# Gates turned and spread over ranks through DRAM, with a transposed down projection, in an attention and mixture-of-adapters kernel

## The chip, the cores and the metric

The kernel runs on one core of a Trainium2 chip. The metric is the device time of one execution in microseconds. Before the change it is 389.1 us, the median of three runs (388.85 to 389.68).

## What is computed

Attention of 49,152 queries over few keys, and then a mixture of eight low-rank adapters on the attention's output. Cut to what matters:

```python
B, N, C = 4, 12288, 128                      # q is (B, N, C), kv is (B, 384, 32, C)
kv_pool = kv averaged over 4 x 4 patches     # 96 x 8 = 768 keys for each of B
k = v = kv_pool @ w_sr
a = softmax(q @ k.T / sqrt(C))
x = (a @ v).reshape(B * N, C)

logits = x @ w_gate                          # E = 8 adapters of rank 16, A (E, C, 16), B (E, 16, C)
top two adapters of each row; w = softmax of their two logits
out = x + sum over the two of w * ((x @ A[e]) @ B[e])
```

## The kernel before

A chunk is 512 queries, taken as four groups of 128; there are 96 chunks, 24 for each of the four batches, and every constant below is of that size (`T = 512`, `S = 4`, `P = 128`, `E = 8`, `RK = 16`, `NB = 24`, `GC = 4`). Ranks and adapters together make 8 x 16 = 128, so all down projections are one 128 x 128 matrix `a_bf`, and all up projections one matrix `b_bf`.

The steps of one chunk, each cut to its core. Scores come with keys on partitions; attending brings queries to partitions. Every matmul, transposes too, is recorded under the helper's line (`L68`), so the profile tells them apart by tile names.

```python
def scores(k, r):        # three times a chunk: 2 x 512 columns, then exp on ScalarE
    ps = ps_s.tile([P, 2, T], FP32, tag="sg")
    for i in range(2):
        mm(ps[:, i], kfT[b][:, 2 * r + i], rhs, ...)
    keep(nc.scalar.activation(em[k][:, 2 * r:2 * r + 2], ps, AF.Exp, ...))

def attend(k, s):        # four times a chunk: 6 matmuls of 137 columns (values, logits, sum)
    ...                  # acc: a PSUM tile of a pool with one buffer

def normalize(k):        # DVE: xn = acc / sum, and so empties acc
def top(k):              # DVE: the eight logits sorted, four MAX8
def route(k0):           # GpSimd, for a pair of chunks: arg and mask of the two chosen

def gates(k0):
    n, eng, arg, mask = routed[k0]                      # eng is GpSimd
    keep(nc.scalar.activation(th, arg, AF.Tanh, bias=0.0, scale=0.5))
    w = gpool.tile([P, GC * S, 8], FP32, tag="gw")      # queries on partitions
    keep(eng.tensor_tensor(w[:, 0:n], th, mask, op=ALU.mult))
    keep(eng.tensor_tensor(w[:, 0:n], w[:, 0:n], mask, op=ALU.add))

def transposes(kx, kh, engine):     # x of one chunk and hg of another, in one PSUM tile
    ps = mtile([P, 2, S, P], BF16, name="tt_ps")
    ...                             # 4 transposes of xn[kx], 4 of hg[kh]
    copy to sb                      # 1024 elements, or 512 where one of the two is absent
    xT[kx], hgT[kh] = sb[:, 0], sb[:, 1]

def down(k):
    hp[k] = mtile([P, S, P], name="h_ps")
    for s in range(S):              # xT is stationary, a_bf moves: queries on partitions
        mm(hp[k][:, s], xT[k][:, s], a_bf, ...)

def gate(k):                        # DVE: hg = hp * gate, the gate repeated over 16 ranks
def up(k):                          # 4 matmuls, hgT stationary, b_bf moving
def finish(k):                      # DVE: d_ps + xn, then the output DMA on SyncE
```

`mtile` takes its tiles from a PSUM pool with two buffers: `tt_ps`, `d_ps`, `h_ps` and the tiles of the key preparation go round in it. The gates use that a softmax of two logits is a tanh of their difference; the factor 0.5 is in `a_bf`.

The slots 14 to 71 are software-pipelined by one function; before and after it stand hand-ordered lists that the change leaves alone. Each engine works in the order in which the program gives it instructions. One slot, in order (`sc` scores, `ga` gates, `nm` normalize, `tt` transposes, `fi` finish, `at` attend, `tp` top, `ro` route, `dn` down, `ge` gate, `lq` the transposing load of four chunks' q on SyncE, `kv` a load of the next batch's keys, `pr` and `pa` its preparation on TensorE and GpSimd, `cq` a cast of q in DRAM, issued by GpSimd after a small copy `late` that waits for an earlier `lq`):

```python
def slot(k):
    if k % GC == 0: lq k // GC + 1
    kv of the next batch (i < 12), cq k // GC + 2 (k % GC == 2)
    sc k 0
    ga k - 4                        # for the first chunk of a pair
    nm k - 2;  tt k - 6, k - 7;  sc k 1;  up k - 8;  fi k - 8
    at k - 1, 0;  tp k - 2;  ro k - 2   # ro after the second of a pair
    sc k 2;  dn k - 6;  ge k - 6
    pr of the next batch
    at k - 1, 1 to 3
    pa of the next batch
```

Of the kernel before, what the change touches and what calls it, by code (L numbers as in the profile page):

```python
# [10 lines left out]
FP32 = mybir.dt.float32  # L11
BF16 = mybir.dt.bfloat16
U16 = mybir.dt.uint16
FP16 = mybir.dt.float16
AF = mybir.ActivationFunctionType
ALU = mybir.AluOpType
# [4 lines left out]
def kernel(  # L21
# [10 lines left out]
    nc = tc.nc  # L32
    P = 128
    B, N, C = q.tensor.shape
    E, RK = 8, 16
# [3 lines left out]
    T = 512  # L39
    S = T // P  # L40
    GC = 4
# [7 lines left out]
    const = ctx.enter_context(tc.tile_pool(name="const", bufs=1))  # L49
# [6 lines left out]
    rpool = ctx.enter_context(tc.tile_pool(name="rpool", bufs=4))  # L56
    gpool = ctx.enter_context(tc.tile_pool(name="gpool", bufs=6))
    run = ctx.enter_context(tc.tile_pool(name="run", bufs=3))
    opool = ctx.enter_context(tc.tile_pool(name="opool", bufs=6))
    qdram = ctx.enter_context(tc.tile_pool(name="qdram", bufs=1, space=bass.MemoryType.DRAM))  # L60
    ps_s = ctx.enter_context(tc.tile_pool(name="ps_s", bufs=2, space=bass.MemoryType.PSUM))
    ps_a = ctx.enter_context(tc.tile_pool(name="ps_a", bufs=1, space=bass.MemoryType.PSUM))
# [2 lines left out]
    keep = tc.keep_in_program_order  # L65

    def mm(*a, **k):
        return keep(nc.tensor.matmul(*a, **k))  # L68

    def mtile(shape, dtype=FP32, name="mb"):  # L70
        return ps_m.tile(shape, dtype, tag="mb", name=name)
# [51 lines left out]
    for item in """  # L123
# [5 lines left out]
        at = [None if x == "-" else int(x) for x in at]  # L129
# [13 lines left out]
    id_f = const.tile([P, P], FP32)  # L143
# [24 lines left out]
    def one(pool):  # L168
        if pool == "mb":
            return mtile([P, T], name="tail_ps")  # L170
        if pool == "acc":
            return ps_a.tile([P, S, 256], FP32, tag="acc", name="acc").rearrange(
                "p a c -> p (a c)")[:, 0:T]
        return ps_s.tile([P, 2, T], FP32, tag="sg", name="sg")[:, 0]

    def move(engine, o, i):
        return keep(nc.scalar.copy(o, i) if engine == "A" else nc.vector.tensor_copy(o, i))
# [129 lines left out]
    em, acc, xn, xg, srt, gw = {}, {}, {}, {}, {}, {}  # L307
    tts, xT, hgT, hp, hg, dp = {}, {}, {}, {}, {}, {}
# [34 lines left out]
    def normalize_half(k, h):  # L343
        if ("r", k) not in xn:
            xn["r", k] = rpool.tile([P, S], FP32, tag="rinv", name="rinv")
        if k // GC not in xg:
# [5 lines left out]
            xn[k][:, 2 * h:2 * h + 2], a[:, :, 0:VC],  # L352
            ri.unsqueeze(2).broadcast_to([P, 2, VC]), op=ALU.mult)))

    sizes = [1, 1] + [2] * (NB * (B - 1) // 2 - 1) + [1] * NB
    first, size = {}, {}
    for n in sizes:
        k0 = len(first)
# [3 lines left out]
    def top(k):  # L362
        k0, m = first[k], k - first[k]
        if k0 not in srt:
            srt[k0] = rpool.tile([P, GC, S, 8], FP32, tag="srt", name="srt")
        for s in range(S):
            keep(nc.vector.max(srt[k0][:, m, s], xn[k][:, s, C:VC]))  # L367

# [2 lines left out]
    def route(k0):  # L371
        n = size[k0] * S
        eng = nc.gpsimd
        m0 = k0 % GC * S
        lg = xg[k0 // GC].rearrange("p m s c -> p (m s) c")[:, m0:m0 + n, C:VC]
        so = srt[k0].rearrange("p m s e -> p (m s) e")[:, 0:n]

        def over(i):
            d = rpool.tile([P, GC * S, 8], FP32, tag=f"over{i}", name=f"over{i}")[:, 0:n]
            keep(eng.tensor_tensor(  # L380
                d, lg, so[:, :, i].unsqueeze(2).broadcast_to([P, n, 8]), op=ALU.subtract))
            return d

        arg, mask = over(0), over(1)
        keep(eng.tensor_tensor(arg, arg, mask, op=ALU.add))
        keep(eng.tensor_scalar(mask, mask, 0.0, None, op0=ALU.is_ge))  # L386
        routed[k0] = (n, eng, arg, mask)

    def gates(k0):
        n, eng, arg, mask = routed[k0]  # L390
        th = rpool.tile([P, GC * S, 8], FP32, tag="th", name="th")[:, 0:n]
        keep(nc.scalar.activation(th, arg, AF.Tanh, bias=0.0, scale=0.5))  # L392
        w = gpool.tile([P, GC * S, 8], FP32, tag="gw", name="gw")
        keep(eng.tensor_tensor(w[:, 0:n], th, mask, op=ALU.mult))  # L394
        keep(eng.tensor_tensor(w[:, 0:n], w[:, 0:n], mask, op=ALU.add))  # L395
        gw[k0] = w
# [30 lines left out]
    def gate(k):  # L427
        k0, m = first[k], k - first[k]
        hg[k] = run.tile([P, S, P], BF16, tag="hg", name="hg")
        keep(nc.vector.tensor_tensor(  # L430
            hg[k].rearrange("p s (e r) -> p (s e) r", e=E),
            hp[k].rearrange("p s (e r) -> p (s e) r", e=E),
            gw[k0][:, m * S:(m + 1) * S].rearrange("p s e -> p (s e)")
            .unsqueeze(2).broadcast_to([P, S * E, RK]), op=ALU.mult))

    def up(k):
        dp[k] = mtile([P, S, C], name="d_ps")
        for s in range(S):
            mm(dp[k][:, s], hgT[k][:, s], b_bf, start=(s == 0), stop=(s == S - 1))
# [146 lines left out]

    def gates_here(k):
        th, mask = routed[k]
        gw[k] = gpool.tile([P, S, E], FP32, tag="gw1", name="gw1")
        keep(nc.vector.scalar_tensor_tensor(gw[k], th, 1.0, mask, op0=ALU.add, op1=ALU.mult))  # L590

    late = const.tile([P, 1], FP32)
    a_bf = const.tile([P, P], BF16)
    b_bf = const.tile([P, C], BF16)

    def adapters():
        keep(nc.vector.tensor_scalar(a_bf, a_f, 0.5, None, op0=ALU.mult))
        keep(nc.vector.tensor_copy(b_bf, b_f))

    def first_casts(watch):  # L600
        keep(nc.gpsimd.tensor_copy(late, watch))
        for g in range(2, 4):
            cast_q(g)
# [7 lines left out]
    def plan(b):  # L611
# [8 lines left out]
        "k2": project_k, "va": project_v, "vb": copy_v, "tu": turn_v,  # L620
        "cs": lambda w: first_casts(q_f[1][:, 15, 0:1]),
        "cab": adapters,
        "lq": load_qT, "cq": next_cast,
        "kv": lambda b, h, r: load_kv(b, h, r, None),
        "pa": lambda b, n: plan(b)[0][n // 8][n % 8](),
        "pr": lambda b, n: plan(b)[1][n](),
        "sc": scores, "at": attend, "nm": normalize, "tp": top, "ro": route, "ga": gates,
        "tt": lambda x, h, e: transposes(x, h, nc.scalar if e == "A" else nc.vector),
        "dn": down, "up": up,
        "ge": lambda k: gate(k) if len(hp[k].shape) == 3 else gate_part(k, 0, S),  # L630
        "fi": lambda k: finish(k) if len(dp[k].shape) == 3 else add_here(k, 0, S),
        "nh": normalize_half, "xb": hold_x, "xt": turn_x, "cx": fetch_x, "hb": hold_h, "ht": turn_h, "ch": fetch_h,
        "o95": hold_acc, "pt": attend_part, "hd": hold_hp, "dn2": down_into, "ge2": gate_part,
        "db": hold_d, "up2": up_part, "af": add_here, "ca": carry, "pd": add_there,
        "lastroute": route_here, "lt": tanh_here, "lg_": gates_here,
    }

    def follow(order):
# [7 lines left out]
    def slot(k):  # L646
        b, i = divmod(k, NB)
        o = []
        if k % GC == 0 and k // GC + 1 < B * NG:
            o.append(f"lq {k // GC + 1}")  # L650
        i0 = 4 if b == 0 else 0
        if b + 1 < B and i0 <= i < i0 + 12:
            o.append(f"kv {b + 1} {(i - i0) // 4} {(i - i0) % 4}")
        if k % GC == 2 and k // GC + 2 < B * NG:
            o.append(f"cq {k // GC + 2}")
        o.append(f"sc {k} 0")
        if first[k - 4] == k - 4:
            o.append(f"ga {k - 4}")
        o += [f"nm {k - 2}", f"tt {k - 6} {k - 7} V", f"sc {k} 1", f"up {k - 8}", f"fi {k - 8}",
              f"at {k - 1} 0", f"tp {k - 2}"]  # L660
        if first[k - 2] + size[k - 2] - 1 == k - 2:
            o.append(f"ro {first[k - 2]}")
        o += [f"sc {k} 2", f"dn {k - 6}", f"ge {k - 6}"]
        prs = (14, 15, 16, 18, 19, 20, 21, 22, 23) if b == 0 else (11, 12, 13, 17, 18, 19, 21, 22, 23)
        if b + 1 < B and i in prs:
            o.append(f"pr {b + 1} {prs.index(i)}")
        o += [f"at {k - 1} {s}" for s in range(1, S)]
        if b + 1 < B and i % 2 == 0 and (8 if b == 0 else 6) <= i <= 20:
            lo, n = ((0, 3, 7, 10, 14, 17, 21)[(i - 8) // 2], 4 if i % 4 else 3) if b == 0 else (
                (i - 6) // 2 * 3, 3)  # L670
            o += [f"pa {b + 1} {m}" for m in range(lo, lo + n)]
        return "; ".join(o)
# [28 lines left out]
    for k in range(14, 72):  # L701
        follow(slot(k))
# [89 lines left out]
```

The softmax here doesn't subtract the row's maximum and nothing guards it: scores larger than these inputs give would overflow.

## Time and profile before

| | before |
|---|---|
| time, median of 3 | 389.1 us |
| span of the profiled run | 387.5 us |
| granted TensorE clock | 0.998 |
| queue of SyncE and its share of the 16 DMA engines | 63.98 MB, 55.8% |
| transposes of hg into tt_ps | 316 |
| multiplies by the gate in the slots, each | 0.691 us, 58 of them |
| copies out of tt_ps of 1024 and of 512 elements, each | 0.691 and 0.419 us |

The span is a little shorter than the time of an execution. Busy time is a sum of instruction times; matmuls are pipelined, so that their recorded durations overlap, and the pace of TensorE is read from the starts of successive groups. A wait row names who waited, and what came last of the things it waited for.

### The profile page before, as it was taken

The page shows a single profiled execution, that of the slowest core. Times are in us where ns is not written, and L with a number is a line of the kernel's source. Part 1 is how long each engine was busy: PE and PEld are TensorE (multiplying, and loading weights), DVE is VectorE, ACT ScalarE, POOL GpSimd, SP SyncE. Part 2 cuts the span into 40 slices and gives each one's busy share as a digit, 9 for nine tenths or more (in the row PEclk, how much of TensorE's full clock was granted, in tenths as well). Part 3 has the DMA queues.
Part 4 walks back from the last instruction along what each step waited for, and adds up shares of the span by engine and source line. Part 5 has one row for each costly group of instructions (what it writes and reads, how often), then busy time and mean ns, then how long its engine had stood idle before and what let it go on. Part 6 is the DMA issues. An engine that isn't in the chain of part 4 may idle for free.

```text
span 387.5 us, 11812 instructions
## 1 busy us (share of the span) xinstructions
PE 378.9 (98%) x4620; PEld 303.8 (78%) x4620; DVE 313.5 (81%) x973; ACT 308.3 (80%) x401; POOL 211.0 (54%) x474
## 2 busy tenths in 40 slices
PE   7899999999999999999999999999999999999994
PEld 4777788888888887888887887888877778788893
DVE  1445688989888888989988889888877687988896
ACT  1688997777687786877788787786879999998964
POOL 0011768987331768777533586877613234545682
PEclk9999999999999999999999999999999999999999
DMA  7998997975596999985579989856745665532245
GB/s 263 413 267 200 295 201 220 285 164 140 136 314 140 255 227 331 234 172 142 119 191 272 305 206 333 200 138 142 156 113 105 128 150 165 111 92 105 81 165 219
DMA packets 70745, 76.47 MB, mean 197 GB/s; under 512 B 49857, under 2 KB 51393, under 8 KB 70337
## 3 DMA queue, kind: packets, MB, share of 16 engines
q1 hardware_dynamic: 69552, 63.98, 55.8%
q0 software_dynamic: 704, 11.54, 17.1%
q8 instruction: 36, 0.59, 0.6%
q10 hardware_dynamic: 432, 0.20, 0.2%
q14 instruction: 21, 0.16, 0.2%
HBM read 50.53 MB, written 36.70 MB: 225 GB/s over the span
## 4 chain that ended last, share of the span: by engine, by line
PE 82%; DMA 8%; POOL 5%; DVE 1%; ACT 1%; issue 1%; SPq 0%; POOLq 0%; DVEq 0%; ACTq 0%
PE acc L68 32%; PE sg L68 29%; PE tt_ps L68 8%; DMA kvr<-in_kv_dram 6%; PE h_ps L68 4%; PE d_ps L68 3%; PE tail_ps L68 3%; DMA qT<-qbf 2%; POOL osb L562 1%; PE v_ps L68 1%; POOL over L380 1%; PE kpT_ps L68 1%; POOL gw L394 1%; ACT em L319 1%; POOL gw L395 1%
## 5 line engine op out<-in xcount | busy, mean ns | idle before, releaser
L319 ACT ACTIVATE em<-sg 128x1024 f16<-128x1024 f32 x288 | 278.3, 1026 | 56.4 <-PE sg L68 55.9
L68 PE MATMUL sg<-qT,kfT 128*128 128x512 bf16 x576 | 169.6, 379 | 0.0
L68 PE MATMUL acc<-vx,em 128*128 128x137 f16 x2280 | 168.9, 223 | 0.0
L68 PEld LDWEIGHTS <-em 128*128 128x128 f16 x2304 | 147.2, 98 | 11.4 <-DVE xn L337 2.7
L68 PEld LDWEIGHTS <-tts 128*128 128x128 bf16 x660 | 49.2, 98 | 31.8 <-issue 0.2
L264 POOL TENSOR_TENSOR kvr<-kvr 128x512 f32<-128x512 f32 x54 | 67.4, 1271 | 0.0
L337 DVE TENSOR_TENSOR xn<-acc,rinv 128x544 f32<-128x544 f32 x83 | 60.1, 724 | 3.2 <-DVE rinv L333 0.3
L380 POOL TENSOR_TENSOR over<-xn,srt 128x64 f32<-128x64 f32 (+1 forms) x114 | 29.8, 282 | 55.2 <-DVE srt L367 55.2
L416 DVE COPY tts<-tt_ps 128x1024 bf16<-128x1024 bf16 (+1 forms) x83 | 53.9, 651 | 4.8 <-PE tt_ps L68 4.6
L394 POOL TENSOR_TENSOR gw<-th,over 128x64 f32<-128x64 f32 (+1 forms) x57 | 16.7, 293 | 63.7 <-ACT th L392 62.7
L68 PEld LDWEIGHTS <-kfT 128*128 128x128 bf16 x576 | 46.1, 98 | 2.8
L430 DVE TENSOR_TENSOR hg<-h_ps,gw 128x512 bf16<-128x512 f32 x58 | 40.1, 691 | 4.5
L68 PEld LDWEIGHTS <-xn 128*128 128x128 bf16 x384 | 28.6, 98 | 18.2
L443 DVE TENSOR_TENSOR osb<-d_ps,xn 128x512 f32<-128x512 f32 x58 | 40.1, 691 | 0.0
L333 DVE RECIPROCAL rinv<-acc 128x4 f32<-128x4 f32 x83 | 15.1, 182 | 29.3 <-PE acc L68 28.6
L68 PE MATMUL tt_ps<-id_bf,xn 128*128 128x128 bf16 x344 | 33.3, 219 | 0.0
L367 DVE MAX8 srt<-xn 128x8 f32<-128x8 f32 x368 | 33.0, 152 | 0.1
L68 PE MATMUL tt_ps<-id_bf,hg 128*128 128x128 bf16 x316 | 30.4, 219 | 0.0
L68 PEld LDWEIGHTS <-hg 128*128 128x128 bf16 x384 | 25.6, 98 | 1.9 <-DVE hg L531 0.3
L68 PE MATMUL h_ps<-a_bf,tts 128*128 128x128 bf16 x264 | 25.5, 219 | 0.0
L68 PE MATMUL d_ps<-b_bf,tts 128*128 128x128 bf16 x260 | 25.1, 219 | 0.0
L386 POOL TENSOR_SCALAR over<-over 128x64 f32<-128x64 f32 (+1 forms) x57 | 19.1, 335 | 5.2
(119 smaller groups left out, 325.3 us busy)
## 6 DMA issues: line engine op xcount, KB each, us to landing
out_dram<-osb SPq DMA_DIRECT2D x91, 256.0 KB, 3.3
kvr<-in_kv_dram SPq DMA_DIRECT2D x45, 512.0 KB, 6.2
qbf<-in_q_dram POOLq DMA_DIRECT2D x22, 512.0 KB, 6.3
kvr<-in_kv_dram SPq DMA_DIRECT2D x6, 256.0 KB, 8.6
out_dram<-osb SPq DMA_DIRECT2D x9, 128.0 KB, 2.1
qf<-in_q_dram SPq DMA_DIRECT2D x4, 256.0 KB, 6.9
qf<-in_q_dram SPq DMA_DIRECT2D x2, 512.0 KB, 8.2
qT<-qbf SPq DMA_TRANSPOSE x22, 5.1
```

The costliest lines, as they stand in the source:

```text
L68: return keep(nc.tensor.matmul(*a, **k))
L264: keep(nc.gpsimd.tensor_tensor(u[:, lo:hi], u[:, lo:hi], v[:, lo:hi], op=ALU.add))
L319: keep(nc.scalar.activation(em[k][:, 2 * r:2 * r + 2], ps, AF.Exp, bias=0.0, scale=scale))
L333: keep(nc.vector.reciprocal(ri, acc[k][:, :, VC]))
L337: keep(nc.vector.tensor_tensor(x, acc[k][:, :, 0:VC], ri.unsqueeze(2).broadcast_to([P, S, VC]), op=ALU.mult))
L367: keep(nc.vector.max(srt[k0][:, m, s], xn[k][:, s, C:VC]))
L380: keep(eng.tensor_tensor(d, lg, so[:, :, i].unsqueeze(2).broadcast_to([P, n, 8]), op=ALU.subtract))
L386: keep(eng.tensor_scalar(mask, mask, 0.0, None, op0=ALU.is_ge))
L394: keep(eng.tensor_tensor(w[:, 0:n], th, mask, op=ALU.mult))
L416: keep(nc.vector.tensor_copy(sb[:, lo:hi], ps[:, lo:hi]))
L430: keep(nc.vector.tensor_tensor(hg[k].rearrange("p s (e r) -> p (s e) r", e=E), hp[k].rearrange("p s (e r) -> p (s e) r", e=E), gw[k0][:, m ...
L443: keep(nc.vector.tensor_tensor(osb, dp[k], xn[k][:, :, 0:C], op=ALU.add))
```

## The change

For 20 chunks, 30 to 41 and 54 to 61, the adapter's inner vector is produced with ranks on partitions from the start, so that it needs no transpose between the two projections. `a_bf` becomes stationary and the transposed x moves through it, in one matmul of 512 columns. The gate then has to lie with ranks on partitions too, and each adapter's gate has to be repeated over 16 partitions. GpSimd writes the gates of a pair as fp16 in the order adapter, group; TensorE transposes them (64 rows); VectorE copies them out; one DMA puts them to DRAM (16 KB); and a second DMA reads each of the eight rows 16 times into 128 partitions (256 KB). A turned chunk's x is transposed one slot later than before, and its output comes in the same slot as before.

```diff
+    turned = {*range(30, 42), *range(54, 62),}
 def gates(k0):
+        if k0 in turned:
+            keep(eng.tensor_tensor(th, th, mask, op=ALU.mult))
+            gh[k0] = gpool.tile([P, E, n], FP16, tag=f"gh{n}", name="gh")
+            keep(eng.tensor_tensor(gh[k0].rearrange("p e m -> p m e"), th, mask, op=ALU.add))
+            return
...
+    def turn_gates(k0, pool, engine):
+        ps = one(pool).bitcast(FP16)[0:n, 0:P]
+        mm(ps, gh[k0].rearrange("p e m -> p (e m)"), id_h, is_transpose=True, start=True, stop=True)
+        gt[k0] = rpool.tile([P, P], FP16, tag="gt", name="gt")[0:n]
+        move(engine, gt[k0], ps)
+
+    def put_gates(k0):
+        gd[k0] = gdram.tile([E, size[k0] * T], FP16, tag=f"gd{size[k0]}", name="gd")
+        keep(nc.sync.dma_start(gd[k0].rearrange("e (m t) -> (e m) t", t=P), gt[k0]))
+
+    def spread_gates(k0):
+        gx[k0] = gxpool.tile([P, GC // 2 * T], FP16, tag="gx", name="gx")[:, 0:n]
+        keep(nc.sync.dma_start(gx[k0], gd[k0].unsqueeze(1).broadcast_to([E, RK, n])))
+
+    def down_turned(k, pool):
+        hp[k] = one(pool)
+        mm(hp[k], a_bf, xT[k].rearrange("p s t -> p (s t)"), start=True, stop=True)
+
+    def gate_turned(k):
+        hgT[k] = run.tile([P, S, P], BF16, tag="hg", name="hg")
+        keep(nc.vector.tensor_tensor(hgT[k].rearrange("p s t -> p (s t)"), hp[k],
+                                     gx[first[k]][:, m * T:(m + 1) * T], op=ALU.mult))
...
 def slot(k):
+        if first[k - 6] == k - 6 and k - 6 in turned:
+            o.append(f"g3 {k - 6}")                       # spread, first thing of the slot
...
+        far, near = k - 7 in turned, k - 6 not in turned
+        x = k - 6 if near else "-"
+        h = "-" if k - 7 in turned else k - 7
+        if (x, h) != ("-", "-"):
+            o.append(f"tt {x} {h} V")
+        if far:
+            o.append(f"tt {k - 7} - V")
...
+        if far:
+            o += [f"dT {k - 7} mb", f"gT {k - 7}"]        # down_turned, gate_turned
+        if near:
+            o += [f"dn {k - 6}", f"ge {k - 6}"]
...
+        o += [f"at {k - 1} {s}" for s in range(1, S - 1)]
+        if first[k - 4] == k - 4 and k - 4 in turned:
+            o += [f"g1 {k - 4} mb V", f"g2 {k - 4}"]      # turn_gates, put_gates
+        o.append(f"at {k - 1} {S - 1}")
```

The start also makes an fp16 copy of the identity (`id_h`), and the scratch tiles of `top`, `route` and `gates` are cut to the pair that they hold.

## The prediction

> **What bounds the kernel now.** I read the busy table of the page first, then the waits of the stretch that the change touches, then that stretch instruction by instruction. The busy table has TensorE at 98%, the others near 80% or less:
>
> ```profile
> PE 378.9 (98%) x4620; PEld 303.8 (78%) x4620; DVE 313.5 (81%) x973; ACT 308.3 (80%) x401; POOL 211.0 (54%) x474
> ```
>
> A busy TensorE can still hide waits, so the second view is the list of waits between 140 and 285 us. That is the stretch in which the slots 34 to 71 run (a slot is one call of slot(k), about one chunk's worth of work):
>
> ```profile
> ACT em L319 <- PE sg L68: 32.9, 39, 1.3
> POOL over L380 <- DVE srt L367: 23.7, 14, 4.2
> POOL gw L394 <- ACT th L392: 19.1, 17, 1.7
> DVE rinv L333 <- PE acc L68: 11.6, 36, 0.6
> POOL late L606 <- DMA qT<-qbf: 3.9, 2, 2.2
> PEld kpT_ps L68 <- POOL kvr L262: 0.3, 1, 0.3
> ```
>
> Each row is waiter, what it waited for, us in total, times, longest. Everybody waits for TensorE; TensorE itself waits once, for 0.3 us. Third, the timeline of slot 34 (start, duration, engine, line):
>
> ```profile
> 142.08 0.59 PE L68 MATMUL sg<-qT,kfT 128*128 128x512 bf16 x2
> 142.51 0.39 PE L68 MATMUL tt_ps<-id_bf,xn 128*128 128x128 bf16 x4
> 142.73 0.39 PE L68 MATMUL tt_ps<-id_bf,hg 128*128 128x128 bf16 x4
> 142.96 0.59 PE L68 MATMUL sg<-qT,kfT 128*128 128x512 bf16 x2
> ...
> 144.40 0.39 PE L68 MATMUL h_ps<-a_bf,tts 128*128 128x128 bf16 x4
> 144.63 1.24 PE L68 MATMUL acc<-vx,em 128*128 128x137 f16 x18
> ...
> 145.71 0.59 PE L68 MATMUL sg<-qT,kfT 128*128 128x512 bf16 x2
> ```
>
> Read starts, not durations, because matmuls overlap. Four transposes of hg take 142.96 - 142.73 = 0.23 us, two 512-column matmuls 0.43, four down projections 144.63 - 144.40 = 0.23, eighteen attend matmuls 1.08 (0.06 each). A slot lasts 145.71 - 142.08 = 3.63 us, which is the sum of its matmuls and nothing else: **columns through TensorE are the bound here**, some 0.055 us per 128.
>
> [...] So one matmul of 512 costs what four of 128 cost, and only removed columns count. [...] the copy of 1024 bf16 out of PSUM takes 691 ns, the multiply of 512 fp32 out of PSUM also 691, so an fp16 second operand shouldn't make the gate multiply faster. [...]
>
> **The change part by part**, for its 20 chunks (10 pairs).
>
> 1. *Transposes of hg gone*: 80 matmuls of 128 columns, 20 x 0.225 = **-4.5 us** of TensorE.
> 2. *Down projection turned*: one matmul of 512 for four of 128: 0.215 against 0.225, **0**.
> 3. *Gates turned*: one 128-column transpose per pair, 10 x 0.06 = **+0.6 us**. Together **-3.9 us**, if nothing new waits.
> 4. *DVE*: the copy shrinks from 1024 to 512 elements, 0.69 to 0.42 us (rows of both forms in the groups by form); per pair one small copy comes, perhaps 0.2. So about -0.17 per chunk, and DVE was not the bound.
> 5. *GpSimd*: same count, fp16 output in the other order, about the same 0.32 us each. *ScalarE*: nothing.
> 6. *DMA*: per pair 16 KB out and 256 KB in. The page has 256 KB landing 3.3 us after issue, 64 KB after 1.8 (weights). They have a slot and a half for the put and two for the spread, and are hidden unless the queue is blocked.
>
> **New waits on TensorE**, which works in program order and now has a GpSimd result in its stream: the transpose of the gates stands before the last attend group of the slot in which GpSimd makes them. In a turned slot it comes 0.43 + 0.22 + 0.43 + 0.22 + 0.36 + 0.43 + 0.22 + 0.72 = 3.03 us after the slot starts. In slot 44, which starts at 180.43, the second gate operation starts at 182.84 and lasts 0.32, so is done 2.73 us in: 0.3 us to spare, and the same sum gives 0.3 in slots 40, 62 and 64. Two slots are worse, because a cast of q waits on GpSimd for a transposing load:
>
> ```profile
> 144.86 0.18 POOL L606 CAST late<-qT 128x1 f32<-128x1 bf16 x1 [2.21 <-DMA qT<-qbf]
> 145.09 0.58 POOL L79 DMA_DIRECT2D qbf<-in_q_dram  x1
> 145.71 0.33 POOL L394 TENSOR_TENSOR gw<-th,over 128x64 f32<-128x64 f32 x1
> 146.12 0.32 POOL L395 TENSOR_TENSOR gw<-gw,over 128x64 f32<-128x64 f32 x1
> ```
>
> - Slot 34: gates ready at 146.12 + 0.32 = 146.44; TensorE gets there at 145.71 - 0.36 = 145.35. It stands for 1.1 us. The 0.3 us wait of slot 35 for GpSimd's key sums then falls away: **+0.8**.
> - Slot 38: slots 35 to 37 come late by that and then save 0.6, so it starts near 158.05 and reaches the transpose at 161.08. The gates were ready at 161.18 + 0.32 = 161.50, after a load that ended at 159.9 and may end a little later beside new DMA: **+0.5**.
> - Slots 48 and 68, where turned and plain chunks meet, hold two transposed inputs. The third PSUM tile of two buffers waits for the first one's copy: DVE ends that 1.50 us into the slot (the copy starts 1.08 in, 0.42 long), TensorE wants it at 1.31: 0.2 each, **+0.4**.
> - Pair 32: the put stands behind a transposing load that held SyncE from 153.77 to 157.70. Put issued near 158.5, landed near 161, spread landed near 164.5; the multiply wants it near 163.5 in slot 39. DVE stands for about 1 us, of which its slack takes most: **+0.3**.
> - Ten small semaphore delays and the extra identity copy: **+0.3**.
>
> Sum: -3.9 + 2.3 = **-1.6 us**. The stages after slot 71 are unchanged and start earlier by it. 389.1 - 1.6 = **387.5 us**.
>
> **Rivals.**
> - *Clean removal*: the waits are absorbed, 385.2 us. For it: DVE and ScalarE have slack and TensorE waited for only 0.3 us. Against: attend work ahead of TensorE can't overtake a waiting transpose.
> - *GpSimd's latency becomes the bound*: the spare time is only 0.3 us. If the fp16 output in the other order costs GpSimd 0.3 us more, or ScalarE's tanh comes later, each pair loses some tenths; with 0.4 in all ten pairs the gain is gone: 389 to 391.
> - *Late spread*: if the spread lands a slot late in several pairs, DVE stops before it empties the single attend accumulator and TensorE follows, up to 1 us a pair: 390 or more. Against: after slot 48 no such blocked queue is seen, and the chunks chosen have their spreads where few keys load.
>
> **Range and chances.** The clean case is the floor, 385.2. Half the ten pairs losing 0.5 us beyond my sum is +2.5, so 390.0. I take 385.3 to 389.9. Over 2% faster means under 381.3, more than all removed columns give: 0.01. Over 2% slower means above 396.9, a wait of over 1 us in every pair: 0.03.
>
> **What would show it.** Matmuls of tt_ps from hg fewer by 80 and slots of about 3.41 us (3.63 - 0.22) confirm step 1. A new row "PE or PEld waits for POOL gh" of about 1.1 us once and 0.4 once confirms the gates' wait; ten times some tenths means the second rival. A row "DVE hg waits for DMA gx" shows the late spread. The copy out of tt_ps at 0.42 and the multiply at 0.69 us confirm step 4. I'd be wrong if TensorE's stream ran into a wait that no view of before shows, such as a blocked SyncE queue delaying the output buffers or the load of q.

## The result, and the profile after

The changed kernel takes **395.5 us** (median; 394.2 to 395.6, and once 400.4) against 389.1 us of the kernel before beside it: ratio 1.0152, 95% interval 1.0123 to 1.0181. The execution of 400.4 ran in a slower state, and the ratios here, which are of means, leave such executions out, so that they can differ a little from what the medians give. The prediction was 387.5, range 385.3 to 389.9: wrong side, outside the range. Four microseconds of TensorE were to go, and six and a half more came.

Busy table of the page after. TensorE, the bound before with 98%, is down to 95% of a longer span, though it has 130 matmuls fewer (by its weight loads, 4490 for 4620; of the matmuls themselves some records are missing):

```profile
PE 375.0 (95%) x4418; PEld 297.9 (76%) x4490; DVE 310.1 (79%) x986; ACT 309.1 (79%) x401; POOL 211.3 (54%) x474
```

Groups by form of the kernel after (line, engine, operation, tiles, count; then busy us, mean ns of one; then idle before it and its releasers). The copy and the multiply cost what was foreseen; GpSimd's fp16 gate costs 478 ns, not 320:

```profile
L426 DVE COPY tts<-tt_ps 128x512 bf16<-128x512 bf16 x36 | 14.6, 415 | 1.2 <-PE tt_ps L70 1.1
...
L469 DVE TENSOR_TENSOR hg<-tail_ps,gx 128x512 bf16<-128x512 f32 x20 | 13.8, 691 | 10.7 <-DMA gx<-gd 7.3 <-PE sg L70 1.7 <-PE tail_ps L70 0.2
...
L401 POOL TENSOR_TENSOR gh<-th,over 128x64 f16<-128x64 f32 x10 | 4.8, 478 | 0.8
```

Waits of the kernel after between 140 and 290 us (waiter, what it waited for; total, times, longest). Where TensorE waited once for 0.3 us, it now waits for the adapter's multiply (the PE and PEld rows), because the multiply waits for the spread gates; and GpSimd's wait for a load of q went from 3.9 to 6.1:

```profile
DVE hg L469 <- DMA gx<-gd: 7.3, 3, 3.3
POOL late L647 <- DMA qT<-qbf: 6.1, 5, 2.1
PEld L70 <- DVE hg L469: 3.7, 2, 2.3
PE d_ps L70 <- DVE hg L469: 2.7, 2, 1.8
...
DVE hg L469 <- PE sg L70: 1.7, 1, 1.7
...
PE tt_ps L70 <- DVE hg L469: 1.3, 2, 0.8
PEld L70 <- POOL gh L401: 1.1, 1, 1.1
PE tail_ps L70 <- POOL gh L401: 0.9, 1, 0.9
```

The spreads that come late are four: those of the pairs 32, 54 and 56 make up the first row, and that of pair 36 hides in the row of PE sg. There the multiply starts at 182.82, as the last packets of a spread issued at 176.60 have run; the score matmul that the row names merely ended about then.

Chain of waits of the kernel after, asked for 140 to 200 us (start, us, what). Before, this chain was a load of q and GpSimd's work behind it until 148.5 us, and from there on nearly all TensorE. Now 20.5 us of it are two puts and two spreads, one after the other, and only then the multiply and TensorE:

```profile
145.48 6.56 DMA gd<-gt
152.06 3.91 DMA gx<-gd
156.06 0.52 DVE hg L469
156.58 3.41 DMA gd<-gt
160.01 6.58 DMA gx<-gd
166.68 0.69 DVE hg L469
167.50 0.73 DVE xn L339
168.28 0.53 PE acc L70 x6
```

SyncE waits for the put ahead of each of the ten spreads, 17.0 us in all and at most 4.0 (waits of SyncE, kernel after), and what stands behind waits too: the first spread is issued at 152.06, when its put has run its 6.56 us, the load of q behind it at 152.94. A put takes 3.4 or 6.6 us, a spread 3.9 or 6.6. What makes the long one long is the question of the experiments. TensorE's timeline of slot 40 shows the damage (start, duration, operation; in brackets idle before it and its releaser). The slot starts at 165.27, should reach its third scores 1.76 us later (as it does without the DMAs), and gets there at 168.65, 1.6 us late:

```profile
165.27 0.59 PE L70 MATMUL sg<-qT,kfT 128*128 128x512 bf16 x2
165.70 0.39 PE L70 MATMUL tt_ps<-id_bf,xn 128*128 128x128 bf16 x4
165.92 0.59 PE L70 MATMUL sg<-qT,kfT 128*128 128x512 bf16 x2
167.43 0.40 PE L70 MATMUL d_ps<-b_bf,hg 128*128 128x128 bf16 x4 [0.91 <-DVE hg L469]
168.28 0.53 PE L70 MATMUL acc<-vx,em 128*128 128x137 f16 x6 [0.45 <-DVE xn L339]
168.65 0.38 PE L70 MATMUL sg<-qT,kfT 128*128 128x512 bf16 x1
```

Up projection waits for the multiply; the next attend waits for the normalization that stands behind the multiply on VectorE and empties the one accumulator.

**Where the time went, by slots.** The length of a slot is the distance between the starts of its first score matmuls on TensorE's timeline. The slots 34 to 48 and 58 to 68 hold all turned chunks; the nine between are alike before and after (32.65 us).

| us | before | after | without put and spread (first experiment below) |
|---|---|---|---|
| slots 34 to 48 | 57.40 | 60.72 | 57.14 |
| slots 58 to 68 | 41.72 | 45.10 | 42.01 |
| of these: slot 38, 62 | 3.63, 3.63 | 4.75, 4.61 | 3.77, 4.00 |
| slot 40, 44, 64 | 3.63, 3.63, 3.63 | 5.38, 4.79, 6.26 | 3.77, 3.78, 3.77 |

Two things stand in this table. After is 6.7 us above before, which is the result. And the kernel without the two DMAs is level with before: so the removed 4.5 us are eaten already without them, and the DMAs bring 6.7 on top, **all of it in five slots**: (4.75 - 3.77) + (4.61 - 4.00) = 1.6 in slots 38 and 62, (5.38 - 3.77) + (4.79 - 3.78) + (6.26 - 3.77) = 5.1 in slots 40, 44 and 64.

Slot 38 stands for the gates (the rows POOL gh). The other four are late spreads. Slot 62 is one too, of pair 54, and no wait for GpSimd (VectorE's and TensorE's timeline of the kernel after):

```profile
250.82 0.69 DVE L469 TENSOR_TENSOR hg<-tail_ps,gx 128x512 bf16<-128x512 f32 x1 [1.55 <-DMA gx<-gd]
251.57 0.38 PE L70 MATMUL tt_ps<-id_bf,xn 128*128 128x128 bf16 x4 [0.58 <-DVE hg L469]
```

That spread was late because its put was slow: the put was issued at 238.85 and the spread could follow only at 246.99, 8.1 us later.

### The profile page after: what moved, and what is told of

The parts are those of the page before. It is cut to its first block, busy times and chain, and to the rows that moved or that the text cites. A ratio compares the mean times of both kernels' runs of the same rounds, so it can differ in the third digit from the quotient of the medians.

```text
span 393.8 us, 11529 instructions
## 1 busy us (share of the span) xinstructions
PE 375.0 (95%) x4418; PEld 297.9 (76%) x4490; DVE 310.1 (79%) x986; ACT 309.1 (79%) x401; POOL 211.3 (54%) x474
## 4 chain that ended last, share of the span: by engine, by line
PE 70%; DMA 13%; DVE 6%; POOL 5%; ACT 3%; issue 2%; SPq 0%; POOLq 0%; DVEq 0%; ACTq 0%
PE acc L70 28%; PE sg L70 22%; PE tt_ps L70 7%; DMA kvr<-in_kv_dram 6%; PE tail_ps L70 5%; DMA gx<-gd 4%; PE d_ps L70 4%; DMA gd<-gt 3%; PE h_ps L70 3%; ACT em L321 2%; POOL osb L598 1%; POOL over L385 1%; DVE rinv L335 1%; PE v_ps L70 1%; DVE xn L339 1%
## 5 line engine op out<-in xcount | busy, mean ns | idle before, releaser
L70 PE MATMUL acc<-vx,em 128*128 128x137 f16 x2280 | 170.7, 223 | 1.3 <-DVE xn L339 0.9
L70 PE MATMUL sg<-qT,kfT 128*128 128x512 bf16 x504 | 154.4, 379 | 0.1
L70 PEld LDWEIGHTS <-tts 128*128 128x128 bf16 x500 | 36.9, 98 | 22.4 <-issue 0.2
L426 DVE COPY tts<-tt_ps 128x1024 bf16<-128x1024 bf16 (+1 forms) x85 | 48.5, 574 | 4.8 <-PE tt_ps L70 4.6
L404 POOL TENSOR_TENSOR gw<-th,over 128x64 f32<-128x64 f32 (+1 forms) x47 | 13.5, 287 | 56.0 <-ACT th L397 55.0
L70 PEld LDWEIGHTS <-hg 128*128 128x128 bf16 x384 | 26.4, 98 | 10.8 <-DVE hg L469 3.7
L440 DVE TENSOR_TENSOR hg<-h_ps,gw 128x512 bf16<-128x512 f32 x38 | 26.2, 691 | 2.8
L70 PE MATMUL tt_ps<-id_bf,hg 128*128 128x128 bf16 x236 | 22.6, 219 | 0.0
L469 DVE TENSOR_TENSOR hg<-tail_ps,gx 128x512 bf16<-128x512 f32 x20 | 13.8, 691 | 10.7 <-DMA gx<-gd 7.3
L390 POOL TENSOR_TENSOR over<-over,over 128x64 f32<-128x64 f32 (+1 forms) x57 | 16.7, 293 | 4.5
```

The lines of the kernel that those rows point to most:

```text
L426: keep(nc.vector.tensor_copy(sb[:, lo:hi], ps[:, lo:hi]))
L440: keep(nc.vector.tensor_tensor(hg[k].rearrange("p s (e r) -> p (s e) r", e=E), hp[k].rearrange("p s (e r) -> p (s e) r", e=E), gw[k0][:, m ...
```

## Experiments

### First: without the DMAs, and with gates that need not be waited for

**Leave out put and spread**; the multiply reads a constant tile of 0.5, so the routing has no effect on the turned chunks' output.

```diff
 def put_gates(k0):
-        (the put)
+        pass
 def spread_gates(k0):
-        (the spread)
+        gx[k0] = gx_c                     # fp16 constant
```

> The change without its two DMAs: the gates are still made, transposed and copied out, but the put and the spread are left out, and the multiply by the gate reads a constant tile (so the output isn't the reference's). If the DMAs are the cause (the spread lands late, and the wait for the put holds up SyncE's queue), 386 to 388: the saved columns of -3.9 us less the gates' wait in slots 34 and 38. If the gates' latency on GpSimd in TensorE's stream is the cause, ten waits stay and it is 391 to 395.

Measured 388.97 us, ratio 1.0012 (0.9997 to 1.0026). The DMAs, with the waits that hang on them, are 6.6 us. But the clean gain doesn't appear either, and TensorE's timeline of this kernel says why in two places. Slot 39, then the end of slot 40:

```profile
162.26 0.52 PE L70 MATMUL acc<-vx,em 128*128 128x137 f16 x6
162.71 0.59 PE L70 MATMUL sg<-qT,kfT 128*128 128x512 bf16 x2
...
166.85 0.88 PE L70 MATMUL acc<-vx,em 128*128 128x137 f16 x12
167.66 0.24 PE L70 MATMUL tail_ps<-id_h,gh 128*64 128x128 f16 x1
167.84 0.53 PE L70 MATMUL acc<-vx,em 128*128 128x137 f16 x6
```

- *End of slot 40*: 12 attend matmuls take 12 x 0.06 = 0.72, so the transpose of the gates could start at 167.57. It starts at 167.66, 0.09 later, and the attend behind it another 0.18 later. So a slot with it takes 3.77 us and one without 3.49: it costs **0.28 us, not 0.06**. No wait row goes with it.
- *Slot 39*: six attend matmuls take 0.36 and the third scores should start at 162.62. They start at 162.71. In the kernel before they come on time:

```profile
162.92 0.52 PE L68 MATMUL acc<-vx,em 128*128 128x137 f16 x6
163.28 0.59 PE L68 MATMUL sg<-qT,kfT 128*128 128x512 bf16 x2
```

  (That is the same slot: 0.36.) With the change TensorE is 0.22 us earlier in the slot than before and the scores' PSUM tile, one of two, isn't free yet: the exp of the slot's first scores starts on ScalarE at 161.64, takes 1.02 us and so reads it until 162.66. So a slot saves 0.13 of its 0.22 us: 3.49 instead of 3.41.

In the profile the gates' transpose has the form 128*64, those of x have 128*128. Two experiments with edits of this kernel, further below, test the width as the cause of the first loss and the wait for the scores' tile as the cause of the second.

**Constant gates for the transpose** (GpSimd's latency taken away; put and spread kept, gates constant):

```diff
-        mm(ps, gh[k0].rearrange("p e m -> p (e m)"), id_h, ...)
+        mm(ps, gh_c[:, 0:n], id_h, ...)
```

> The change with the transpose of the gates reading a constant tile: TensorE no longer waits for GpSimd, which still does its work; put, spread and all else stay in place (the output isn't the reference's). If the late DMAs are the cause, the three late spreads stay, some 6 us of the losses, and only about 2.5 us comes back: 392 to 394. If the gates' latency is the cause: 386 to 388.

395.38 us, 1.017 (1.0133 to 1.0208): no help, and the 2.5 us that were expected back didn't come. TensorE waits for no gate now. The profile, of the slowest execution (397.6 us), has VectorE wait for the spread more, not less, and slots 38 and 68 now lose to late spreads as well (5.81 and 6.81 us; waits of this kernel, 130 to 290 us):

```profile
DVE hg L470 <- DMA gx<-gd: 9.5, 4, 3.3
```

**GpSimd's latency as the bound falls.**

**A spread that doesn't wait for the put.** It reads a DRAM tile filled once at the start; the put still runs, and nobody reads it.

```diff
-        keep(nc.sync.dma_start(gx[k0], gd[k0].unsqueeze(1).broadcast_to([E, RK, n])))
+        keep(nc.sync.dma_start(gx[k0], gd_c.unsqueeze(1).broadcast_to([E, RK, n])))
```

> The change with the spread reading a DRAM tile that was filled once at the start, so that it doesn't wait for its put; the puts stay (the output isn't the reference's). If what counts is that the wait for the put holds up SyncE's queue (late spread, late load of q behind it, so a late cast and late gates), nearly all comes back: 387 to 389. If a spread is slow by itself, because a cast holds the DMA engines or because its source of eight rows is slow to read, little comes back: 392 to 395.

391.2 us, 1.0055 (1.0037 to 1.0072); in the profile, of the fastest execution (389.2 us), slots 40 and 64 are back at 3.77. The bytes are the same and were moved; so 4.3 of the 6.6 us hang on the *wait*, and on the moment at which it lets a spread be issued, not on the traffic.

### Second: what makes a spread late

In the trace, three of the four late spreads were issued just behind a cast of q (the fourth, of pair 54, follows the slow put). GpSimd's timeline of the kernel after, around the spread at 160.01 of the chain above:

```profile
159.46 0.18 POOL L647 CAST late<-qT 128x1 f32<-128x1 bf16 x1 [2.06 <-DMA qT<-qbf]
159.68 0.58 POOL L81 DMA_DIRECT2D qbf<-in_q_dram  x1
160.29 0.33 POOL L399 TENSOR_TENSOR th<-th,over 128x64 f32<-128x64 f32 x1
160.70 0.47 POOL L401 TENSOR_TENSOR gh<-th,over 128x64 f16<-128x64 f32 x1
```

(The same lines show slot 38's loss: the gates stand behind `late`, which waits 2.06 us for q; TensorE stands 0.91 us at their transpose, the row POOL gh above.) And the packets on the 16 DMA engines:

```
160.0 - 160.5 us   SyncE's queue: 2 packets of 2,048 B
160.5 - 162.5 us   cast: 16 pieces of 32,768 B begin, 3.0 to 3.5 us each
                   SyncE's queue: nothing
162.5 - 164.0 us   nothing new begins
164.0 us on        SyncE's queue: 2,048 B packets, mostly 84 ns each
```

Between two of its packets, at 160.17 and 164.13 us, SyncE's queue begins none for 4.0 us. The packets show this pause, not what makes it.

**Cut the cast into small pieces**: its DRAM tile padded so that rows aren't contiguous.

```diff
-        t = qdram.tile([GT, C], BF16, ...)
+        t = qdram.tile([P, w + 64], BF16, ...)[:, 0:w]      # w = GT // P * C
```

> The change with the DRAM tile of the cast q padded, so that a cast is 128 pieces of 4 KB in place of 16 of 32 KB, computing the same. The trace of the changed kernel has each 32 KB piece hold its DMA engine for 3.3 us, and the three late spreads stand behind such pieces. If this holding up is the cause of the late spreads, they land some 3 us earlier: 390 to 392. If the wait for the put is the cause, or the reading of eight rows, no more than 1 us changes: 394 to 396.

395.42 us, 1.0131 (1.0063 to 1.0199). The times, from 391.7 to 397.4, don't decide; the trace does. Pieces of 4,096 B of 0.32 to 1.2 us replace the big ones, and still SyncE's queue moves nothing from 160.5 to 164.0 us. **For this late spread, that big pieces are the cause falls.** But the block is no rule. In the same kernel the cast issued at 142.22, while keys loaded, had its pieces between 146.2 and 150.8 us, and SyncE's queue moved packets all through, with no pause over 0.12 us; in 32 KB pieces that cast (146.2 to 149.4 in the kernel after) left it a pause of 1.8 us.

**Move the casts** behind the gates of the slot, so that gates don't stand behind `late`; and, in the second, also issue them a group earlier:

```diff
-        cq k // GC + 2  at the slot's start
+        cq k // GC + 2  behind ga           # second: k // GC + 3, and late copies qT[g - 3]
```

> The change with one thing moved: in the slots that issue a cast of q, GpSimd makes the gates first and then waits for its load and issues the cast. It computes the same. If the late spreads come from a cast that starts together with them (all 16 DMA engines then carry the cast for 3 us or more), the spread now goes out some 2 us ahead of the cast, and the gates of these slots are ready on time: 391 to 392.5. If the wait for the put on SyncE's queue is what makes them late, the order on GpSimd matters little: 394 to 396.

> As the run with the cast after the gates, and in the slots each cast is also issued a group of four chunks earlier, so that no load of q waits for its cast. If casts and loads that wait for each other around the put and spread are the cause, this frees SyncE's queue too: 389 to 391. If the put's own landing time is the cause, 393 or more.

396.77 us, 1.0207 (1.0178 to 1.0236), and 395.87 us, 1.0167 (1.015 to 1.0184). Neither helps; what was forecast for casts as the cause, 391 to 392.5 and 389 to 391, failed both times. In the first the put of pair 30 took 8.9 us and slot 38 6.27, so the next spread (162.43) was behind its cast (162.14) once more. The chain of the second, same stretch:

```profile
146.45 7.42 DMA gd<-gt
...
153.89 3.89 DMA gx<-gd
...
158.39 3.54 DMA gd<-gt
...
161.96 5.86 DMA gx<-gd
```

The cast was issued at 145.36 here, now just ahead of the first *put*, which takes 7.4 us instead of 6.6; that makes all behind it later, and the second spread is behind the next cast (160.79) again.

**The casts a group earlier, at their old place in the slot, in the kernel before**:

> The kernel before with the casts of the last run in this list alone. TensorE waits for only 0.3 us in the slots of the kernel before, so earlier casts can bring no more than that: 388.5 to 389.5. If casts matter by themselves, under 388.5 or over 390.

389.14 us, 1.0002 (0.9994 to 1.001): earlier casts change nothing in the kernel before, where no put and spread wait.

**The put on ScalarE's queue**, so that it isn't behind SyncE's other work:

```diff
-        keep(nc.sync.dma_start(gd[k0].rearrange(...), gt[k0]))
+        keep(nc.scalar.dma_start(gd[k0].rearrange(...), gt[k0]))
```

> The change with one thing moved: the ten puts are issued by ScalarE on its own DMA queue, the spreads stay on SyncE's. It computes the same. In the trace of the changed kernel the put of the first pair of each group of turned chunks stands behind loads of keys on SyncE's queue and lands 6.6 to 8 us after its issue; SyncE waits for it, and with it the load of q and the next pair's put. If this is where the late spreads begin, the first puts now land in 2 to 3 us and the losses of the slots 38 to 44 and 62 to 64 go: 389.5 to 391.5. If a put is slow for another reason (the write to DRAM itself, or the casts), 394 or more.

391.44 us, 1.007 (1.0039 to 1.01), 4.1 better. It is worth seeing what it does *not* do. SyncE's timeline of this kernel:

```profile
152.13 0.71 SPq L460 DMA_DIRECT2D gx<-gd  x1
153.02 2.81 SPq L86 DMA_TRANSPOSE qT<-qbf  x1
...
157.87 0.64 SPq L460 DMA_DIRECT2D gx<-gd  x1
```

The first put left at 145.91, and its spread follows at 152.13: 6.2 us, so another queue hardly speeds that put (6.6 before). The first put of the other group did get faster, 5.5 us instead of 8.1, and slot 62 is clean (3.77). And the second put leaves ScalarE at 153.82, while on SyncE it stood behind that transposing load of q until 156.58:

```profile
145.48 0.52 SPq L455 DMA_DIRECT2D gd<-gt  x1
...
152.06 0.70 SPq L460 DMA_DIRECT2D gx<-gd  x1
152.94 2.92 SPq L86 DMA_TRANSPOSE qT<-qbf  x1
155.95 0.53 SPq L480 DMA_DIRECT2D out_dram<-osb  x1
156.58 0.53 SPq L455 DMA_DIRECT2D gd<-gt  x1
```

(SyncE's timeline of the kernel after.) So the second spread leaves at 157.87, just ahead of the cast at 158.31.

**The first pairs of each group plain** (16 chunks turned instead of 20; the groups' slow first puts fall away):

```diff
-    turned = {*range(30, 42), *range(54, 62),}
+    turned = {*range(32, 42), *range(56, 62),}
```

> The change with the first pair of each group left as before (chunks 32 to 41 and 56 to 61 turned), so that no put is issued while keys load. It computes the same. If the late spreads begin with the first pair's put behind the loads of keys, what follows is on time and the time is that of the run with puts on ScalarE's queue: 390 to 392. If the casts are the cause, the later pairs lose as before: 393.5 to 395.5.

391.94 us, 1.0063 (1.0039 to 1.0086): 3.6 better with less of the change. Slots 40 and 68 still lose (4.59 and 5.70 us), each to a spread behind a cast.

**Cast or spread first: one table over the runs.** Issue times from the timelines, for the pairs 32 and 56. All runs with the DMAs, but for those that turn 54 chunks, put the spread on ScalarE's queue or give it one slot more:

| | pair 32: cast, spread | slot 40 | pair 56: cast, spread | slot 64 |
|---|---|---|---|---|
| after | 159.68, 160.01 | 5.38 | 252.88, 253.64 | 6.26 |
| constant gates | 161.88, 162.16 | 5.80 | 253.24, 254.37 | 5.28 |
| cast in small pieces | 159.45, 159.78 | 5.29 | 251.75, 252.33 | 8.69 |
| cast after gates | 162.14, 162.43 | 5.66 | 254.44, 254.66 | 5.72 |
| cast after gates, a group earlier | 160.79, 161.96 | 6.35 | 253.46, 253.72 | 6.24 |
| put, wide gates, early cast (below) | 157.28, 157.88 | 5.15 | 248.34, 248.73 | 5.79 |
| first pairs plain | 158.35, 158.68 | 4.59 | 249.02, **247.84** | 3.77 |
| spread not after put | 158.13, **156.89** | 3.77 | 249.09, **246.77** | 3.77 |
| put on ScalarE | 158.31, **157.87** | 3.77 | 250.01, **249.56** | 3.77 |
| put, wide gates (below) | 160.72, **157.65** | 3.46 | 249.22, **248.77** | 3.46 |
| all three (below) | 160.53, **158.32** | 3.46 | 250.16, **249.01** | 3.46 |

Bold is a spread ahead of its cast, by 0.4 us or more: nine, and none costs anything. Thirteen are behind, by 0.2 to 1.2 us, and each makes its slot 4.59 or longer. The third late one of the kernel after, in slot 44, was issued at 176.60 behind a cast at 176.03. One case lies between: with the put on ScalarE the spread of pair 36 was issued at 173.85, 0.21 us ahead of a cast at 174.06, took 6.8 us all the same, and slot 44 took 4.65.

The spreads of the pairs 36, 40 and 60 share a slot with a cast too. With them, 19 spreads of these runs were issued behind a cast, and 18 made VectorE wait; the one that didn't (pair 36 with constant gates, 0.58 us behind) happened to have 6.0 us until it was needed. Of 36 issued ahead, only two came late: the one above, and pair 40 with the first pairs plain, 0.09 us ahead (slot 48: 4.41 instead of 4.06). So some tenths of a microsecond decide, in a race between two engines' queues. No run moved a single cast and nothing else, so this rests on the order of issue over eleven kernels. It doesn't explain why times of one kernel differ so much: without put and spread they lie between 388.4 and 393.3 too.

### Third: the two costs without DMAs

**Gates padded to 128 columns**, without put and spread, and **down projection ahead of the third scores**, without put and spread:

```diff
+    gh_p = [three constant [P, P] fp16 tiles, zeroed; the gates fill 64 columns]
-        ps = one(pool).bitcast(FP16)[0:n, 0:P]
-        mm(ps, gh[k0].rearrange("p e m -> p (e m)"), id_h, is_transpose=True, ...)
+        ps = one(pool).bitcast(FP16)[:, 0:P]
+        mm(ps, gh_t[k0], id_h, is_transpose=True, ...)
```

```diff
-        sc k 2;  dT k - 7;  gT k - 7
+        dT k - 7;  gT k - 7;  sc k 2
```

> The run without put and spread, with the gates' tile padded from 64 to 128 columns before its transpose (so the weights are of full width; the multiply still reads a constant). In the trace of the run without put and spread a transpose of 64 gate columns takes 0.28 us of TensorE's time in place of the 0.06 that I counted. If that comes from weights of less than full width, ten of them give back 2.1 us: about 386.8. If it is a wait or belongs to any transpose put between attend matmuls, it stays at 389.

> The run without put and spread, with the turned down projection put ahead of the third pair of scores in place of after it (the multiply still reads a constant). In the trace of the run without put and spread the third pair of scores starts 0.09 us late in every turned slot, and its PSUM tile is the one that ScalarE's first exp of the slot has to free. If TensorE has thus run into ScalarE, the moved matmul fills the gap, and 20 slots give 1.8 us: about 387.2. If the gap has another cause it stays at 389.

387.69 us, 0.997 (0.9954 to 0.9986), and 388.14 us, 0.9982 (0.9968 to 0.9996), against 388.97 without either. With 128 columns the turned slot with gates goes from 3.77 to 3.54 us and slot 34, which has only the transpose of gates added, from 3.91 to 3.68, which is 3.63 + 0.05: **a wider transpose is 0.23 us cheaper**. The runs show the cost by width, not what causes it: padding also widens what is written from 64 to 128 partitions. With the down projection first, turned slots go from 3.60 to 3.51, 3.49 to 3.40 and 3.77 to 3.68: the 0.09 us come back, and 3.40 is the full saving.

### Fourth: versions that keep the gates and might win

Each of these computes the full result. Put on ScalarE, padded gates and down projection first (first row), with the casts a group earlier at their old place (second) or behind the gates (third), that third with the spread on ScalarE's queue as well, and that with 54 chunks turned:

```diff
+ the edits above together; spread on ScalarE's queue: nc.sync becomes nc.scalar, placed behind ga
+    turned = {*range(10, 64)}            # the last one
```

> The change with the puts on ScalarE's queue, the gates padded to 128 columns, and the turned down projection ahead of the third scores; casts as in the change. It computes the same. 391.4 of the run with the puts moved, less 10 x 0.21 and less 18 x 0.09 that the two other terms have measured: about 388, so just under the kernel before. If the shorter slots make more spreads late, 390 or more.

> As the run before it in this list, with each cast of q in the slots a group earlier and at its old place in the slot, ahead of the gates. The cast then never waits for a load of q and starts just behind the spread of its slot. If the casts' late start takes the rest, 386 to 387.5; if the cast now stands before a put or a spread, 389 or more.

> The change with all that the runs so far point to, computing the same: gates padded to 128 columns for their transpose (-2.1 us), the turned down projection ahead of the third scores (-1.8), casts after the gates and a group earlier, puts on ScalarE's queue. If the three causes add up, this is what I first predicted for the clean removal: 385 to 387. If spreads are still late, 388 to 391.

> As the run with all three mended, with the spread too on ScalarE's queue, after the first exp of its slot. If SyncE's wait for the put is all that is left, this is a little faster, 385 to 386.5; if ScalarE then waits for the put and so holds up its exps, or the later spread comes too late, slower: 388 or more.

> As the run with put and spread on ScalarE's queue, with the chunks 10 to 63 turned, also those taken while keys load. 27 pairs at 2 x 0.225 - 0.06 = 0.39 us each are 10.5 us of TensorE's columns: about 379 if nothing waits. If the loads of keys make the puts or spreads late there, as the choice of chunks in the change supposes, the waits take the gain: 388 to 400.

| | us | ratio (95%) |
|---|---|---|
| put, wide gates, down first | 389.59 (386.1 to 391.7) | 1.001 (0.9992 to 1.0027) |
| with early casts | 392.47 | 1.0089 (1.0065 to 1.0113) |
| with early casts behind the gates | 390.43 | 1.0024 (1.001 to 1.0037) |
| spread on ScalarE's queue too | 398.81 | 1.0238 (1.0202 to 1.0275) |
| 54 chunks so | 430.0 | 1.1094 (1.1027 to 1.1161) |

The best ties with the kernel before. Its slots 40 and 64 are clean, but slot 38 takes 6.06 us: TensorE waits 1.6 us for the gates, which stand behind the copy that waits for q, and before that 0.5 us for the late spread of pair 30 (GpSimd's timeline of it):

```profile
160.49 0.18 POOL L653 CAST late<-qT 128x1 f32<-128x1 bf16 x1 [3.37 <-DMA qT<-qbf]
```

Moving the casts behind the gates takes that away and puts a cast in front of a later put instead (chain of that kernel):

```profile
252.09 8.00 DMA gd<-gt
...
260.11 3.61 DMA gx<-gd
```

With the spread on ScalarE's queue, ScalarE itself stands waiting for the put, and TensorE runs out of exp (waits, 130 to 290 us; with 54 chunks turned so, VectorE waits for 13 spreads, 22.9 us in all):

```profile
PE sg L70 <- ACT em L321: 6.9, 4, 2.0
...
ACT em L321 <- DMA gd<-gt: 2.7, 1, 2.7
```

**One slot more for the spread**: everything from the transpose of x on a slot later in turned chunks; alone, and with put on ScalarE, padded gates, down first and casts behind the gates.

```diff
-        far, near = k - 7 in turned, k - 6 not in turned
+        far, near = k - 8 in turned, k - 6 not in turned      # and k - 8 for up, finish: k - 9
```

> The change with transpose of x, turned down projection, multiply and up projection of a turned chunk all one slot later, so that a spread has 3.6 us more until it is needed; gates, put, spread and casts are as in the change. It computes the same. If the spreads' lateness is all that the DMAs cost, this is the time of the run without put and spread, 389 to 390, or a little more for the two slots with double work at the end of each group. If the DMAs cost time in another way (gates late behind a cast, output stores held up), 391 or more.

> All together, computing the same: one slot later, gates padded to 128 columns, turned down projection ahead of the third scores, puts on ScalarE's queue, casts in the slots after the gates. From the run without put and spread (389.0), less 2.1 for the padded gates and less 1.3 to 1.6 for the order of down projection and scores, plus up to 1 for the ends of the groups: 386 to 387.5. If late gates or DMAs remain, 388 or more.

395.27 us, 1.0165 (1.015 to 1.0181), and 391.05 us, 1.0056 (1.0042 to 1.0069). In the first the wait for the spread is gone from the list altogether, though its spreads stand behind casts as before (160.62 and 160.99). What took its place:

```profile
PEld L70 <- POOL gh L401: 3.8, 2, 1.9
...
PE tail_ps L70 <- POOL gh L401: 3.5, 2, 1.7
```

TensorE stands for gates that come behind `late` in slots 38 and 58, some 1.8 us each, and the slots where a group ends hold double work: the two after slot 48 take 4.35 + 4.14 us instead of 3.63 + 3.63, the two after slot 68 5.37 + 4.73 instead of 3.90 + 4.15, together 3.3 us. In the second kernel these four take 4.35, 4.14, 5.24 and 4.73. So a slot of slack does hide the late spread, and costs as much elsewhere.

## Why the prediction was wrong, step by step

- **Steps 1 and 2 (transposes of hg gone, down projection turned)**: the count is right (80 fewer, one matmul of 512 at 0.215). But a slot is 3.49, not 3.41. What failed here is to read "ScalarE: nothing": its exp wasn't slower (1.02 us each before and after), but TensorE, once faster by 0.22 us, meets its buffer. Putting the down projection first won back 0.8 us in all.
- **Step 3 (gates turned, +0.6)**: mis-sized. 10 x 0.28 = 2.8 for a transpose of 64 columns, which I had counted like one of 128. Padding alone won 1.3 us between the medians; the slots of its profile, of its fastest execution, are 2.2 shorter.
- **Step 4 (VectorE)**: right: 0.415 for the copy, and 0.691 for the multiply with its fp16 second operand.
- **Step 5 (GpSimd)**: 0.48 for 0.32 in one of the two operations. Without the DMAs TensorE stands 0.2 us for gates once, in slot 62.
- **Waits for GpSimd** (+0.8 in slot 34, +0.5 in slot 38): slot 34 didn't wait at all (3.63 + 0.28 = 3.91): its cast, which stands ahead of the gates, was issued at 142.24 and not at 145.09. Slot 38 waited 1.0 (4.75 against 3.77), but without the DMAs it doesn't wait: the cast ahead of its gates goes out at 157.62 and not at 159.68.
- **Slots 48 and 68**: both 4.06 with the DMAs and without. Their work is 3.63 + 0.22 for a second down projection, so the wait is 0.2 each, as foreseen.
- **Step 6 and pair 32's late spread (+0.3)**: this is the miss. I had the mechanism: the put behind the transposing load on SyncE, expected at 158.5, seen at 156.58, and landed by 160.0 instead of 161. But I gave the spread 3.5 us, from the page's median for transfers of its size, and it took 6.6, being issued 0.33 us behind a cast. And it happened three times, for pairs 32, 36 and 56, 5.1 us in all; pair 54's spread, whose put took 8.1 us, cost 0.6 more: 5.7 us instead of 0.3. So the step that failed is that the two transfers "are hidden unless the queue is blocked" within a slot and a half for the put and two for the spread. A put of 8.1 us and spreads that took 6.2 to 7.1 us until the multiply could start didn't fit. The page's median from issue to landing, 3.3 us for 256 KB, was no bound for it.

Together, without the DMAs I'd have had -1.6 - 0.3 = -1.9 and measured about 0: +2.2 for the gates' transpose, some +1 for the exp buffer, and about -1 of GpSimd waits that didn't come. With them, +6.7 more. The third rival, a late spread, was right in kind: it named 390 or more, and I argued it away because no queue is blocked after slot 48. Two of the four late ones cost slots before it, 40 and 44, and the other two, in slots 62 and 64, come from a slow put and from a cast.

Left open: why a cast keeps SyncE's queue still in one place and not in another (at 160 us it isn't the size of its pieces); why the puts of the pairs 30 and 54 take 5.5 to 9.3 us on either queue (casts and key loads were both under way); why, with the spread on ScalarE's queue, the spread of pair 30 took 6.8 us with no cast issued within 8 us of it; and how the versions of the fourth group would fare with a cast placed by time and not by slot, which wasn't tried.

## What to carry to other kernels

Before a new short DMA goes on the critical path, list what else may be issued around it, above all casts by GpSimd, and plan with its time behind those, not with its median (here 6.6 us behind a cast, where 3.5 was planned). When work is taken off the bounding engine, look for the buffer that the next engine frees last: it may give back only part (here 0.13 of 0.22 us a slot). Transposing half a tile can cost more than a whole one, as it did here (0.28 us for 64 columns, 0.05 for 128).

## What the runs showed of the hardware

- A transpose with 64 weight columns cost 0.28 us of TensorE's time, with 128 columns 0.05.
- Behind a DRAM-to-DRAM cast of 512 KB issued at 159.68 (159.45 with small pieces), SyncE's queue began no packet for 4.0 us, in pieces of 32 KB and of 4 KB alike. Behind another, with key loads under way, its longest pause was 1.8 us with 32 KB and 0.1 us with 4 KB.
- Where VectorE's multiply waited for a 256 KB spread on SyncE's queue, it began 5.7 to 8.8 us after the issue if the spread was issued 0.2 to 1.2 us behind a cast, and 3.7 to 4.8 us, once 5.9, if no cast was issued within 5 us.
- A 16 KB put and the start of its spread lay 2.2 us apart at the quickest, 3.4 in the chain above, and 6.6 and 8.1 us in the kernel after where a cast had been issued 3.2 and 2.5 us before and keys were loading.
- GpSimd's multiply or add of 64 elements took 318 to 323 ns with contiguous fp32 output, and 478 with fp16 output in the strided order; type and order weren't tried apart.
